# A hand-planned attention and MoE kernel: v loaded in two pieces in the last batch, the planner's rule for adding transfers, and the order of the last matmuls

## The chip, the core and the metric

The kernel runs on one core of a Trainium2 chip. Its engines work side by side: TensorE (PE) multiplies matrices, VectorE (DVE) and ScalarE (ACT) work on tiles, GpSimd (POOL) and SyncE (SP) here mostly start transfers. Each engine takes its own instructions in the order in which the program gives them. The metric is the time of one execution in microseconds (us), and the program computes everything in float32 accuracy, most products split into a high and a low part.

## The reference, cut to what matters

```python
def _attn_ref(q, k, v, tau):            # B, N, C = 4, 6080, 256
    qn = q / (np.linalg.norm(q, axis=1, keepdims=True) + 1e-06)
    kn = k / (np.linalg.norm(k, axis=1, keepdims=True) + 1e-06)
    s = kn.transpose(0, 2, 1) @ qn / tau
    a = softmax(s)                      # over the last axis, written out
    return v @ a

def _moe_ref(x, w_in, w_out):           # x: all 24320 rows; 256 -> 2048 -> 256
    h = x @ w_in
    g = h - np.tanh(h)
    return g @ w_out
```

## The kernel before, in words

**Stages.** There are four batches. Attention is over the 256 channels, so a batch's softmax gives a 256 x 256 matrix, which is multiplied into w_in once (the "folded" factors f, kept in DRAM as f_d). After that every batch is only h = f v, g = h - tanh(h), out = w_out g. The 6080 columns of v make six pairs of two chunks (512 and 512, one pair 512 and 448); the 2048 hidden rows make eight quads. A step of the main loop is one quad of one pair: names such as `c11_3_2_1` are the operand, batch 3, pair 2, quad 1. While a batch runs, the scores of the next are worked out beside it.

**Products of a quad.** A quad multiplies 2 x 2 blocks by a scheme with seven products instead of eight (p1 to p7 in `Quad.product`). Each product is three matmuls of 512 columns (low and high parts). The results gather in PSUM in X, Y and Z: p1 starts X, and p6, p7 and p4 add to X one after the other. Between these, ScalarE copies X out (p1, u2, u3, line L1151), VectorE adds (c11, c22, c12, line L1161: c11 = p1 + Z), then come tanh, the subtraction from h, and the split into a high part (ACT) and a low part (DVE). PE may not add the next product to X before ScalarE has copied it. In the last batch, from pair 1 on ("halves"), Y and Z share a PSUM bank, so that p5 (writes Y) has to wait until c11 has read Z.

**v.** A pair's v comes as four rows of 512 columns per partition (`Moving.load`, L926, tile vraw, one buffer). From it seven operands are made: v0, v2 and v6 are copies of the rows 0, 3 and 2, the others are made from sums (tile vt). Each is split by a CAST on ACT (L952) and a subtraction on DVE (L955). For pairs 2 to 5 of the last batch the load is put at the start of quad 1 of the pair ahead.

**Adding transfers ("joins").** In the last batch the subtraction h - tanh(h) of two results per quad (n11 and t12) is not done by DVE: ACT writes -tanh(h), and a transfer that POOL starts adds h to it (L1176, L1281).

**Second products.** The finished g tiles go into a list, `stream`, and their matmuls (w_out g) are taken from it between the products of later quads. The tables ORDER, UNEVEN and HALVES say how many (a number counts matmuls of 512 columns) behind which product; `lag` says how many are held back. What is left at the end is sorted once more: entries of the last LAST quads that belong to the second chunk go last. Then the outputs are copied out of PSUM and stored.

**The planner.** All this is not run in the order of the code. `plan.add` notes each operation with its engine, a cost, what it reads and writes and, with `after`, the matmul behind which it may start. `Plan.order` then plays the operations through with these costs: PE in its given order, the others by who can start first and whose result is due first, SP's transfers through one modelled queue ("DMA"). The start times that come out set the order of the instructions on every engine. The waits themselves are put in afterwards from the tiles that an instruction really touches; a wrong cost makes a late order, not a wrong result.

Two or three places in this planner matter here. For a load, a reader is held to see its data `LONG_LAG` after the modelled queue is through with it. For an adding transfer, a reader is held to see it JOIN_LAG after its issue, and the queue is occupied for JOIN_SHARE. And a reader depends only on the buffers that stand in its `reads`.

Of the kernel before, what the change touches and what calls it, by code (L numbers as in the profile page):

```python
# [18 lines left out]
P = 128  # L19
# [22 lines left out]
UNEVEN = [  # L42
    ("p6", [2]), ("p2", ["c"]), ("p5", []), ("p7", [12]), ("p3", ["a"]), ("p4", ["d", 3]), ("p1", ["b", 7]),
]
HALVES = [
    ("p6", []), ("p2", [5, "c"]), ("p5", []), ("p7", [5]), ("p4", ["d", 3]), ("p3", ["a", 4]), ("p1", ["b", 5.5]),
]
HALF = NMAX // 2
LAST = 1
SHARE = 1  # L50
JOINED = [(),(11,12)]
SUMS_AT = 3 * 8
ENTER = 10
EARLY = 6
FILLS = 35
# [45 lines left out]
class Plan:  # L101
# [9 lines left out]
    FILL = 0.1  # L111
    WAIT, URGENT, FRONT = 0.35, 2.0, 140.0
    LONG_LAG, BUSY = 4.5, 180.0
    JOIN_LAG, JOIN_SHARE = 4.5, 1.45

    def __init__(self):
        self.ops = []
# [42 lines left out]
    def order(self):  # L160
        ops = self.ops
        for op in reversed(ops):
            if op.due is None:
                op.due = 1e9
            for d in op.deps:
                if d.engine != "PE" or d.fill:
                    d.due = min(1e9 if d.due is None else d.due, op.due - d.cost - self.LAG[d.engine] - self.HOP - d.lag)
        waits = [len(op.deps) for op in ops]
        known = [0.0] * len(ops)
        for op in ops:  # L170
            for d in op.deps:
                d.then.append(op)

        pe = [[op for op in ops if op.engine == "PE" and op.fill == fill] for fill in (False, True)]
        at = [0, 0]
        free = dict.fromkeys(self.ENGINES + ("port", "DMA"), 0.0)
        ready = {e: [op for op in ops if op.engine == e and not waits[op.i]] for e in self.ENGINES if e != "PE"}

        def start(op):
            t = max(free[op.engine], known[op.i])  # L180
            if op.port:
                t = max(t, free["port"])
            if op.engine == "SP":
                t = max(t, free["DMA"] - self.DMA_DEPTH / self.DMA_RATE)
            for b in op.allocs:
                held = b.ring.held
                n = sum(1 for x in op.allocs[:op.allocs.index(b)] if x.ring is b.ring)
                k = len(held) + n - b.ring.bufs
                if k >= 0:
                    if k >= len(held) or held[k].left:  # L190
                        return None
                    t = max(t, held[k].free)
            return t

        done = []
        while len(done) < len(ops):
            best = None
            for i, row in enumerate(pe):
                if at[i] < len(row) and not waits[row[at[i]].i]:
                    op = row[at[i]]  # L200
                    t = start(op)
                    if t is not None and (best is None or t < best[0] - self.FILL):
                        best = (t if i else max(t, min(known[op.i] + op.late, t + op.late)), float(i), op.i)
            for e, some in ready.items():
                can = [(t, op.due, op.i) for op in some for t in [start(op)] if t is not None]
                if can:
                    first = min(can)[0]
                    c = min((c for c in can if c[0] <= first + 1e-9), key=lambda c: c[1:])
                    soon = min((x for x in can if x[0] <= first + self.WAIT), key=lambda c: c[1:])
                    if soon[1] < c[1] - self.URGENT and soon[1] > self.FRONT and e != "SP":  # L210
                        c = soon
                    if best is None or c < best:
                        best = c
            assert best is not None, [(e, len(x)) for e, x in ready.items()]
            op = ops[best[2]]
            op.start = best[0]
            end = free[op.engine] = op.start + op.cost
            seen = end + self.LAG[op.engine] + self.HOP + op.lag
            if op.engine == "SP":
                free["DMA"] = max(free["DMA"], end) + op.size / self.DMA_RATE  # L220
                seen = free["DMA"] + (self.DMA_LAG if op.start < self.BUSY else self.LONG_LAG)
            if op.lag:
                free["DMA"] = max(free["DMA"], end) + self.JOIN_SHARE
            if op.port:
                free["port"] = end
            for b in op.allocs:
                b.ring.held.append(b)
                b.free = seen
            for b in op.reads:
                b.left -= 1  # L230
                b.free = max(b.free, seen)
            if op.engine == "PE":
                at[op.fill] += 1
            else:
                ready[op.engine].remove(op)
            for x in op.then:
                waits[x.i] -= 1
                if op.engine != x.engine or op.engine == "SP" or op.lag:
                    known[x.i] = max(known[x.i], seen)
                else:  # L240
                    known[x.i] = max(known[x.i], end if op.engine == "PE" else end + self.LAG[op.engine] + self.SELF)
                if not waits[x.i] and x.engine != "PE":
                    ready[x.engine].append(x)
            done.append(op)
        return sorted(done, key=lambda op: (op.start, op.i))
# [6 lines left out]
def dve_cost(n):  # L252
    return 0.068 + n * 0.001042
# [11 lines left out]
def attn_moe(ctx: ExitStack, tc: tile.TileContext, qk, v4, qkT, tau, w_in, w_out, outT):  # L265
# [42 lines left out]
    def sb(pool, tag, shape, dtype, name):  # L308
        return pool.tile(list(shape), dtype, tag=tag, name=name, bufs=ring[tag].bufs)
# [42 lines left out]
    class Convert:  # L352
# [5 lines left out]
        def load(self):  # L358
            self.raw = sb(qk_p, "raw", [P, 2, WN], I32, f"raw_{self.name}")
            self.h, self.l = self.dst()  # L360
            nc.sync.dma_start(self.raw, self.src)
# [550 lines left out]
    class Moving:  # L912
# [7 lines left out]
            self.n = self.ns[0]  # L920
            self.hi, self.lo = {}, {}

        def load(self):
            n, s0 = self.n, self.s0
            self.raw = sb(v_p, "vraw", [P, 4, NMAX], F32, f"vraw_{self.b}_{self.p}")
            nc.sync.dma_start(self.raw[:, :, 0:n], v4[self.b, :, 2 * s0:2 * s0 + 4 * n].rearrange("p (a n) -> p a n", a=4))  # L926

        def sums(self, i):
            n = self.n
# [156 lines left out]
    moving = {}  # L1086
    vbuf = {}

    def plan_moving(i, after=()):
        v = moving[i] = Moving(i // NP, i % NP)  # L1090
        n = v.n
        raw, t = Buf(ring["vraw"]), Buf(ring["vt"])
        plan.add("SP", 0.35, v.load, writes=[raw], after=after, size=1.05)
        for j in range(3):
            plan.add("DVE", dve_cost(n if j else 2 * n), lambda j=j: v.sums(j), reads=[raw], writes=[t])
        vbuf[i] = {}
        for j in range(7):
            h = Buf(ring[v.tag(j)])
# [395 lines left out]
        if gs % SLOTS >= NS2:  # L1494
            task(gs - 2, "start", lambda gs=gs: load_folded(gs))
    for i in range(1, B * NP):
        task(NS2 * i - (NS2 - 1 if halved(i // NP, i % NP) and i % NP > 1 else 5), "start", lambda i=i: plan_moving(i, [plan.last_pe]))

    def plan_softmax(a, sq, ps):

# [284 lines left out]
    for gs in range(TOTAL):  # L1785
# [4 lines left out]
        if halves_from - 4 <= gs < halves_from:  # L1790
            lag += 3
        if gs == halves_from:
            lag += 2
        if before and not uneven:
            lag += ENTER if gs < halves_from else 0
            stream[-2:] = reversed(stream[-2:])
# [83 lines left out]
```

## Time and profile before

| | before |
|---|---|
| median of the runs | 2145.4 us (lowest 2145.1) |
| the profiled execution | 2144.87 us |
| its span, first to last instruction | 2143.1 us |
| PE busy | 2135.9 us, 10026 matmuls |
| DVE busy | 1879.0 us |
| ACT busy | 1616.3 us |
| POOL busy | 106.2 us |
| DMA, mean over the span | 196 GB/s |

The profile names each engine's busy time as a share of the span and, for each wait, the instruction or transfer that ended last before the waiting one could go. Matmuls overlap in their pipeline, so that their listed durations (some 0.39 us) are longer than the distance from one start to the next (0.23 us for 512 columns); for the pace of PE the starts are to be read. The same holds on ACT and DVE in a smaller measure: a cast of 512 columns is listed with 0.62 us, and the next one starts 0.52 us later.

### The profile page before, as it was taken

What the parts mean: (1) busy time and instruction counts of PE and PEld (TensorE: products, weight loads), DVE (VectorE), ACT (ScalarE), POOL (GpSimd) and SP (SyncE); (2) the same over time, 40 slices, a digit from 0 to 9 for tenths busy, and PEclk for the clock granted to TensorE, in tenths of its full rate; (3) what the DMA queues carried; (4) which work ended last, traced back from release to release, by engine and by line L of the source; (5) the groups of instructions that cost most, each with busy time, mean ns of one, the idle gap of its engine ahead of it and who ended that gap; (6) DMA issues with size and microseconds to landing.
All of it is one profiled execution on the core that took longest, in us unless ns stands there. A gap on an engine that the chain in (4) does not pass through costs nothing.

```text
span 2143.1 us, 29494 instructions
## 1 busy us (share of the span) xinstructions
PE 2135.9 (100%) x10026; PEld 1802.5 (84%) x10026; DVE 1879.0 (88%) x3332; ACT 1616.3 (75%) x3015; POOL 106.2 (5%) x117
## 2 busy tenths in 40 slices
PE   9999999999999999999999999999999999999999
PEld 8888888888888888888888888888888888888887
DVE  8998988998898888888899888888888998988987
ACT  6677878767777787886777788887676777777776
POOL 5100000000000000000000000000000011111111
PEclk9999999999999999999999999999999999999999
DMA  9845676555335575643533567564353467877874
GB/s 384 303 165 194 214 253 222 189 181 184 127 135 187 212 245 212 219 162 108 199 138 126 180 231 246 196 227 158 110 197 125 156 207 204 230 230 205 231 209 136
DMA packets 143897, 419.73 MB, mean 196 GB/s; under 512 B 20674, under 2 KB 62914, under 8 KB 140674
## 3 DMA queue, kind: packets, MB, share of 16 engines
q1 hardware_dynamic: 132226, 396.87, 52.5%
q0 software_dynamic: 11520, 20.98, 5.4%
q8 instruction: 79, 1.29, 0.2%
q14 instruction: 72, 0.59, 0.1%
HBM read 329.19 MB, written 66.85 MB: 185 GB/s over the span
## 4 chain that ended last, share of the span: by engine, by line
PE 99%; DMA 1%; DVE 0%; SPq 0%; ACT 0%; issue 0%; ACTq 0%
PE ps_o L1448 43%; PE x L326 25%; PE y L326 12%; PE z L326 7%; PE ps_h L1371 5%; PE ps_s L326 3%; PE ps_s L653 2%; PE ps_s L651 1%; PE ps_w L326 1%; DMA n<-c 0%; DMA vhl<-qk_dram 0%; DVE c L1161 0%; DVE t L1285 0%; DVE v L955 0%; DVE gl L1293 0%
## 5 line engine op out<-in xcount | busy, mean ns | idle before, releaser
L326 PE MATMUL x<-v,f 128*128 128x512 f32 (+1 forms) x2304 | 628.2, 389 | 0.0
L1448 PE MATMUL ps_o<-gh,wo_h 128*128 128x512 f32 (+1 forms) x1376 | 533.6, 388 | 0.0
L1448 PE MATMUL ps_o<-gh,wo_l 128*128 128x512 f32 (+1 forms) x1376 | 533.5, 388 | 0.0
L326 PEld LDWEIGHTS x<-v,f 128*128 128x128 f32 x2304 | 430.1, 188 | 84.5
L1293 DVE TENSOR_TENSOR gl<-t,gh 128x512 fp32r<-128x512 f32 (+1 forms) x688 | 456.1, 679 | 20.9 <-ACT gh L1289 19.9
L1289 ACT CAST gh<-t 128x512 fp32r<-128x512 f32 (+1 forms) x688 | 412.2, 617 | 34.4 <-DVE t L1285 20.9
L1448 PE MATMUL ps_o<-gl,wo_h 128*128 128x512 f32 (+1 forms) x1376 | 428.0, 388 | 0.0
L1278 ACT ACTIVATE t<-c 128x512 f32<-128x512 f32 x536 | 333.8, 625 | 94.2 <-DVE c L1161 85.1
L1285 DVE TENSOR_TENSOR t<-c,t 128x512 f32<-128x512 f32 (+1 forms) x496 | 333.9, 677 | 24.7 <-ACT t L1278 19.5
L1151 ACT COPY u<-x 128x512 f32<-128x512 f32 (+1 forms) x384 | 221.9, 578 | 163.0 <-PE x L326 159.4
L1161 DVE TENSOR_TENSOR c<-u,y 128x512 f32<-128x512 f32 (+1 forms) x384 | 258.9, 674 | 76.3 <-ACT u L1151 47.9
L326 PE MATMUL y<-v,f 128*128 128x512 f32 (+1 forms) x1152 | 320.6, 387 | 1.1 <-DVE c L1161 1.0
L1448 PEld LDWEIGHTS ps_o<-gh,wo_l 128*128 128x128 f32 x1376 | 258.5, 188 | 51.4 <-DVE ob L1471 0.9
L1448 PEld LDWEIGHTS ps_o<-gl,wo_h 128*128 128x128 f32 x1376 | 258.2, 188 | 51.7 <-DVE gl L1293 0.6
L1448 PEld LDWEIGHTS ps_o<-gh,wo_h 128*128 128x128 f32 x1376 | 258.4, 188 | 49.1
L326 PEld LDWEIGHTS y<-v,f 128*128 128x128 f32 x1152 | 210.2, 188 | 36.2 <-DVE c L1161 1.8
L1161 DVE TENSOR_TENSOR c<-p,z 128x512 f32<-128x512 f32 x192 | 131.7, 686 | 36.3 <-PE z L326 33.5
L326 PE MATMUL z<-v,f 128*128 128x512 f32 x576 | 162.2, 390 | 0.0
L1278 ACT ACTIVATE t<-x 128x512 f32<-128x512 f32 x152 | 90.9, 598 | 92.7 <-PE x L326 91.1
L1285 DVE TENSOR_TENSOR t<-x,t 128x512 f32<-128x512 f32 x152 | 104.9, 690 | 45.4 <-ACT t L1278 44.9
L326 PEld LDWEIGHTS z<-v,f 128*128 128x128 f32 x576 | 108.1, 188 | 23.3 <-DVE t L1285 0.2
L1151 ACT COPY p<-x 128x512 f32<-128x512 f32 x192 | 112.7, 587 | 15.3 <-PE x L326 12.5
(215 smaller groups left out, 2191.4 us busy)
## 6 DMA issues: line engine op xcount, KB each, us to landing
f<-f_d SPq DMA_DIRECT2D x160, 896.0 KB, 4.6
raw<-qk_dram SPq DMA_DIRECT2D x104, 384.0 KB, 5.0
nt<-qkT_dram SPq DMA_DIRECT2D x96, 380.0 KB, 5.1
f_d<-f SPq DMA_DIRECT2D x32, 896.0 KB, 3.9
vraw<-v_dram SPq DMA_DIRECT2D x24, 1024.0 KB, 7.9
outT_dram<-ob SPq DMA_DIRECT2D x88, 256.0 KB, 3.2
sl<-so_d SPq DMA_DIRECT2D x40, 512.0 KB, 3.3
wt<-wt_d SPq DMA_DIRECT2D x24, 512.0 KB, 6.8
```

Of the source, the lines that this page charges most:

```text
L326: ins = nc.tensor.matmul(out, w, x, start=first and i == 0, stop=last and i == len(seq) - 1, skip_group_check=True,)
L651: nc.tensor.matmul(self.ps[:, 0:C], x[:, 1, k], x[:, 0, q], start=False, stop=last, skip_group_check=True)
L653: nc.tensor.matmul(self.ps.rearrange("p (a c) -> p a c", a=2), x[:, 0, k], x[:, :, q], start=first, stop=False, skip_group_check=True,)
L1151: nc.scalar.copy(self.tiles[to], self.tiles["X"][:, 0:n])
L1161: nc.vector.tensor_add(self.tiles[i], self.tiles[u], self.tiles[ps][:, 0:n])
L1278: nc.scalar.activation(self.tiles["t", i], self.tiles[c][:, 0:n], AF.Tanh, scale=-1.0 if apart else 1.0)
L1285: nc.vector.tensor_sub(x, self.tiles[c][:, 0:n], x)
L1289: nc.scalar.copy(self.g[i][0], self.tiles["t", i])
L1293: nc.vector.tensor_sub(self.g[i][1], self.tiles["t", i], self.g[i][0].bitcast(F32))
L1371: nc.tensor.matmul(outs[b, p, place][:, at_ * HALF:(at_ + 1) * HALF], weights(a, part), quad.g[name][x][:, half * HALF:(half + 1) * HALF], ...
L1448: nc.tensor.matmul(outs[key + (m,)][:, 0:n], (wo_l if part else wo_h)[:, f, m * P:(m + 1) * P], quad.g[i][x], start=first and j == 0, stop ...
```

## The change

It has five parts. (1) In the planner, a reader of an adding transfer is held to see it no earlier than JOIN_AFTER = 2.8 behind the modelled queue's end. (2) For pairs 2 to 5 of the last batch v is loaded in two transfers of two rows each: the first at the start of quad 1 of the pair ahead, the second at the start of quad 2. The operations that make the seven operands are planned with the second (`plan_split`). (3) In the table HALVES half a matmul is moved from behind p4 to behind p2, and `lag` grows by 3 instead of 2 at the start of the halves. (4) LAST is 2 instead of 1. (5) SUMS_AT is 32 instead of 24: the sums of w_out's blocks are made in pair 4 of the first batch instead of pair 3.

```diff
-    ("p6", []), ("p2", [5, "c"]), ("p5", []), ("p7", [5]), ("p4", ["d", 3]), ("p3", ["a", 4]), ("p1", ["b", 5.5]),
+HALVES = [("p6",[]),("p2",[5.5,"c"]),("p5",[]),("p7",[5.0]),("p4",["d",2.5]),("p3",["a",4]),("p1",["b",5.5])]
-LAST = 1
+LAST = 2
+PARTS = [(1,"start"),(2,"start")]
-SUMS_AT = 3 * 8
+SUMS_AT = 32
-    JOIN_LAG, JOIN_SHARE = 4.5, 1.45
+    JOIN_LAG, JOIN_SHARE, JOIN_AFTER = 4.5, 1.45, 2.8
             if op.lag:
                 free["DMA"] = max(free["DMA"], end) + self.JOIN_SHARE
+                seen = max(seen, free["DMA"] + self.JOIN_AFTER)
...
-        def load(self):
+        def load(self, i, k):
             n, s0 = self.n, self.s0
-            self.raw = sb(v_p, "vraw", [P, 4, NMAX], F32, f"vraw_{self.b}_{self.p}")
-            nc.sync.dma_start(self.raw[:, :, 0:n], v4[self.b, :, 2 * s0:2 * s0 + 4 * n].rearrange("p (a n) -> p a n", a=4))
+            if i == 0:
+                self.raw = sb(v_p, "vraw", [P, 4, NMAX], F32, f"vraw_{self.b}_{self.p}")
+            nc.sync.dma_start(
+                self.raw[:, i:i + k, 0:n], v4[self.b, :, 2 * s0 + i * n:2 * s0 + (i + k) * n].rearrange("p (a n) -> p a n", a=k)
+            )
...
-        plan.add("SP", 0.35, v.load, writes=[raw], after=after, size=1.05)
+        plan.add("SP", 0.35, lambda: v.load(0, 4 // parts), writes=[raw], after=after, size=1.05 / parts)
+        vparts[i] = v, raw, t, [Buf(f"vraw{i}_{k}") for k in range(1, parts)]
+        if parts == 1:
+            plan_split(i)
+
+    def plan_part(i, k, after):
+
+        v, raw, t, more = vparts[i]
+        n = 4 // (len(more) + 1)
+        plan.add("SP", 0.35, lambda: v.load(k * n, n), writes=[more[k - 1]], after=[*after, raw.writers[0]], size=1.05 / (len(more) + 1))
+        if k == len(more):
+            plan_split(i)
+
+    vparts = {}
+
+    def plan_split(i):
+        v, raw, t, more = vparts[i]
+        n = v.n
         for j in range(3):
-            plan.add("DVE", dve_cost(n if j else 2 * n), lambda j=j: v.sums(j), reads=[raw], writes=[t])
+            plan.add("DVE", dve_cost(n if j else 2 * n), lambda j=j: v.sums(j), reads=[raw, *more], writes=[t])
         vbuf[i] = {}
         for j in range(7):
             h = Buf(ring[v.tag(j)])
             l = Buf(f"vl{i}_{j}", h)
             src = t if v.PLACES[j][0] else raw
             plan.add("ACT", act_cost(v.width(j)), lambda j=j: v.split_hi(j), reads=[src], writes=[h])
...
-        task(NS2 * i - (NS2 - 1 if halved(i // NP, i % NP) and i % NP > 1 else 5), "start", lambda i=i: plan_moving(i, [plan.last_pe]))
+        late = halved(i // NP, i % NP) and i % NP > 1
+        parts = PARTS if late else [(NS2 - 5, "start")]
+        for k, (at_, place) in enumerate(parts):
+            task(
+                NS2 * (i - 1) + at_, place,
+                lambda i=i, k=k, n=len(parts): plan_part(i, k, [plan.last_pe]) if k else plan_moving(i, [plan.last_pe], n),
+            )
...
         if gs == halves_from:
-            lag += 2
+            lag += 3
```

Every matmul of the kernel before is in the kernel after. Three places show how the rows move.

**ScalarE, last batch, pair 2, around quad 2.** `v0`, `v2`, `v6` with `_3_3` are the operands of the next pair's v; `u2`, `u3` are the copies of X between the products; `n11`, `t22`, `t12` are tanh; `ghb1`, `gh22` and the other CASTs are high parts. Before:

```order
L1151 COPY p1_3_2_2_19077<-x_3_2_2_19065 128x512
L1209 CAST ghb1_3_2_1_19086<-n11_3_2_1_19002 128x256
L1278 ACTIVATE t22_3_2_1_19091<-c22_3_2_1_19027 128x512
L952 CAST v0_3_3_19101<-vraw_3_3_18972 128x512
L1151 COPY u2_3_2_2_19108<-x_3_2_2_19065 128x512
L1289 CAST gh22_3_2_1_19113<-t22_3_2_1_19091 128x512
L1209 CAST t1_3_2_1_19123<-ts_3_2_1_19081 128x512
L1173 ACTIVATE n11_3_2_2_19134<-c11_3_2_2_19117 128x512
L952 CAST v2_3_3_19140<-vraw_3_3_18972 128x512
L1278 ACTIVATE t12_3_2_1_19148<-c12_3_2_1_19058 128x512
L1151 COPY u3_3_2_2_19155<-x_3_2_2_19065 128x512
```

After:

```order
L1171 COPY p1_3_2_2_19076<-x_3_2_2_19065 128x512
L1298 ACTIVATE t22_3_2_1_19086<-c22_3_2_1_19027 128x512
L1298 ACTIVATE t12_3_2_1_19094<-c12_3_2_1_19059 128x512
L1171 COPY u2_3_2_2_19102<-x_3_2_2_19065 128x512
L1229 CAST ghb1_3_2_1_19109<-n11_3_2_1_18997 128x256
L1309 CAST gh22_3_2_1_19115<-t22_3_2_1_19086 128x512
L955 CAST v0_3_3_19125<-vraw_3_3_18971 128x512
L955 CAST v2_3_3_19136<-vraw_3_3_18971 128x512
L955 CAST v6_3_3_19144<-vraw_3_3_18971 128x512
L1193 ACTIVATE n11_3_2_2_19147<-c11_3_2_2_19112 128x512
L1171 COPY u3_3_2_2_19153<-x_3_2_2_19065 128x512
```

The three casts of v, which were spread (v6 came behind u3), stand together now, ahead of n11 and u3.

**SyncE's queue at the same place.** `f` is a quad's folded factor, `sl` sums of w_out's blocks, `outT_dram` the output of the pair ahead. Before:

```order
L909 DMA f_163_18969<-f_d3_3_17364 128x1792
L926 DMA vraw_3_3_18972<-v4_dram 128x2048
L494 DMA sl_161_19000<-so_d1_116 128x1024
L1474 DMA outT_dram<-ob_3_1_1_1_19032 128x512
L1474 DMA outT_dram<-ob_3_1_1_0_19048 128x512
L1403 DMA outT_dram<-ob_3_1_0_18998 128x512
L1403 DMA outT_dram<-ob_3_1_1_19034 128x512
L909 DMA f_164_19099<-f_d3_4_17472 128x1792
L494 DMA sl_162_19138<-so_d2_117 128x1024
```

After:

```order
L909 DMA f_163_18964<-f_d3_3_17364 128x1792
L927 DMA vraw_3_3_18971<-v4_dram 128x1024
L494 DMA sl_161_19006<-so_d1_116 128x1024
L1494 DMA outT_dram<-ob_3_1_1_1_19048 128x512
L1494 DMA outT_dram<-ob_3_1_1_0_19046 128x512
L1423 DMA outT_dram<-ob_3_1_0_19004 128x512
L1423 DMA outT_dram<-ob_3_1_1_19034 128x512
L909 DMA f_164_19092<-f_d3_4_17472 128x1792
L927 DMA vraw_3_3_18971<-v4_dram 128x1024
L494 DMA sl_162_19138<-so_d2_117 128x1024
```

The first piece has the place of the whole load, and the second stands behind the four stores and the next f.

**VectorE, last batch, pair 1, around quad 2.** `ts` and `glb1` read the joined tile n11 of quad 1; c11 of quad 2 is the addition that frees the bank of Z. Before:

```order
L1234 TENSOR_TENSOR ts_3_1_1_18131<-n11_3_1_1_18056 128x256
L1234 TENSOR_TENSOR ts_3_1_1_18131<-n21_3_1_1_18105,n11_3_1_1_18056 128x256
L1285 TENSOR_TENSOR t22_3_1_1_18136<-c22_3_1_1_18080,t22_3_1_1_18136 128x512
L1214 TENSOR_TENSOR glb1_3_1_1_18156<-n11_3_1_1_18056,ghb1_3_1_1_18145 128x256
L1214 TENSOR_TENSOR t1_3_1_1_18150<-ts_3_1_1_18131,t1_3_1_1_18150 128x512
L1161 TENSOR_TENSOR c11_3_1_2_18169<-p1_3_1_2_18127,z_3_1_2_18152 128x512
```

After:

```order
L1305 TENSOR_TENSOR t22_3_1_1_18131<-c22_3_1_1_18082,t22_3_1_1_18131 128x512
L1254 TENSOR_TENSOR ts_3_1_1_18150<-n11_3_1_1_18054 128x256
L1181 TENSOR_TENSOR c11_3_1_2_18160<-p1_3_1_2_18126,z_3_1_2_18145 128x512
L1234 TENSOR_TENSOR glb1_3_1_1_18170<-n11_3_1_1_18054,ghb1_3_1_1_18157 128x256
L1313 TENSOR_TENSOR gl22_3_1_1_18178<-t22_3_1_1_18131,gh22_3_1_1_18163 128x512
```

c11 was the sixth of these rows and stands behind one reader of n11 now.

## Rows read from the trace of the kernel before

**Rows 1.** The page, busy time: us, share of the span, instructions.
```profile
PE 2135.9 (100%) x10026; PEld 1802.5 (84%) x10026; DVE 1879.0 (88%) x3332; ACT 1616.3 (75%) x3015; POOL 106.2 (5%) x117
```

**Rows 2.** All of PE's listed waits: us in total, times, longest.
```profile
PE idle L1823 <- DVE ones L318: 1.1, 1, 1.1
PE y L326 <- DVE c L1161: 1.0, 1, 1.0
PE ps_s L326 <- DMA vhl<-qk_dram: 0.5, 1, 0.5
```

**Rows 3.** The chain that ended last, in order of time: start, us, what.
```profile
1740.28 7.21 DMA n<-c
```

**Rows 4.** Timeline of PE, 1748 to 1755: start, us, instruction, [idle before <- releaser].
```profile
1749.06 0.40 PE L1371 MATMUL ps_h<-t,wo_h 128*128 128x256 f32 x2
1750.47 0.96 PE L326 MATMUL y<-v,f 128*128 128x512 f32 x3 [1.00 <-DVE c L1161]
...
1753.23 0.84 PE L326 MATMUL x<-v,f 128*128 128x512 f32 x3
```

**Rows 5.** Timeline of SP's issues, 1814 to 1833: start, us of issuing.
```profile
1824.60 1.35 SPq L1474 DMA_DIRECT2D outT_dram<-ob  x2
1827.14 0.81 SPq L1403 DMA_DIRECT2D outT_dram<-ob  x2
1828.05 0.41 SPq L909 DMA_DIRECT2D f<-f_d  x1
1831.18 0.33 SPq L494 DMA_DIRECT2D sl<-so_d  x1
```

**Rows 6.** Line L909, the one f issued at 1828.05.
```profile
DMA to landing us min/median/max: 5.4/5.4/5.4
```

**Rows 7.** Line L494, the one sl issued at 1831.18.
```profile
DMA to landing us min/median/max: 3.5/3.5/3.5
```

**Rows 8.** Line L494, the one sl issued at 1725.05, directly behind an f.
```profile
DMA to landing us min/median/max: 5.2/5.2/5.2
```

**Rows 9.** Line L909, the one f issued at 1744.0, behind four stores.
```profile
L909 SPq DMA_DIRECT2D f<-f_d x1: 799/799/799, 1744.0 to 1744.0; - x1
...
DMA to landing us min/median/max: 6.8/6.8/6.8
```

**Rows 10.** Line L494, the one sl issued at 1811.0, alone.
```profile
DMA to landing us min/median/max: 3.2/3.2/3.2
```

**Rows 11.** Timeline of ACT, 1827.5 to 1834.
```profile
1829.54 0.59 ACT L1151 COPY u<-x 128x512 f32<-128x512 f32 x1
...
1831.06 0.63 ACT L1173 ACTIVATE n<-c 128x512 f32<-128x512 f32 x1
1831.59 0.61 ACT L952 CAST v<-vraw 128x512 fp32r<-128x512 f32 x1
...
1832.81 0.59 ACT L1151 COPY u<-x 128x512 f32<-128x512 f32 x1
```

**Rows 12.** Timeline of PE, 1831 to 1835: the products on v4 (p7) and v5 (p4).
```profile
1831.92 0.85 PE L326 MATMUL x<-v,f 128*128 128x512 f32 x3
...
1833.88 0.84 PE L326 MATMUL x<-v,f 128*128 128x512 f32 x3
```

**Rows 13.** Timeline of all engines, the end.
```profile
2137.54 0.39 PE L1448 MATMUL ps_o<-gl,wo_h 128*128 128x512 f32 x1
...
2137.99 0.42 DVE L1400 TENSOR_TENSOR ob<-eh,s 128x256 f32<-128x256 f32 x1
...
2138.33 0.69 DVE L1471 COPY ob<-ps_o 128x512 f32<-128x512 f32 x1
...
2139.26 0.84 SPq L1474 DMA_DIRECT2D outT_dram<-ob  x2
```

**Rows 14.** Stretches behind the last matmul: us, busy (PE, PEld, DVE, ACT, POOL), granted clock, DMA.
```profile
2138.70:2142.60 3.90, 0.00 (x0) 0.00 (x0) 0.32 (x1) 0.53 (x1) 0.00 (x0) 1.00 0.70 269
2142.70:2143.10 0.40, 0.00 (x0) 0.00 (x0) 0.00 (x0) 0.00 (x0) 0.00 (x0) 0.50 0.00 0
```

More of the change, by code (lines that the diff above doesn't have):

```diff
@@ L44 @@
 ]
-HALVES = [
-    ("p6", []), ("p2", [5, "c"]), ("p5", []), ("p7", [5]), ("p4", ["d", 3]), ("p3", ["a", 4]), ("p1", ["b", 5.5]),
-]
+HALVES = [("p6",[]),("p2",[5.5,"c"]),("p5",[]),("p7",[5.0]),("p4",["d",2.5]),("p3",["a",4]),("p1",["b",5.5])]
 HALF = NMAX // 2
-LAST = 1
+LAST = 2
 SHARE = 1
 JOINED = [(),(11,12)]
-SUMS_AT = 3 * 8
+PARTS = [(1,"start"),(2,"start")]
+SUMS_AT = 32
 ENTER = 10
@@ L1087, in attn_moe, with plan_moving @@
     vbuf = {}
-    def plan_moving(i, after=()):
+    def plan_moving(i, after=(), parts=1):
         v = moving[i] = Moving(i // NP, i % NP)
```

## Prediction

> **What bounds the kernel now.** I read first the busy times: TensorE (PE) works through the whole span of 2143.1 us [rows 1]. Busy is not the same as never waiting, so I read next what PE waited for: three waits long enough to be listed, 2.6 us in all, two of them at the start-up (on the constant `ones` and on the first rows of q and k) [rows 2]. From there to the last batch PE waits for nothing, so no other engine's work there has a price as long as it stays hidden. The third wait is in the last batch. The chain of work shows what led to it: an adding transfer (n<-c) that took 7.21 us from its issue at 1740.28 [rows 3]. VectorE and ScalarE work strictly in their order, both had an instruction on that transfer's result at the head, and the addition that PE needed stood behind it: PE's last ps_h matmuls started at 1749.06, about 0.25 us of work, and the next product only at 1750.47, 1.2 us late [rows 4]. That, and the last stores after the last matmul, is all that can be gained. The number of matmuls does not change.
>
> **A wait that goes.** In the order shown for VectorE, the addition c11 of quad 2 now stands right behind the first instruction on the joined tile and ahead of the other readers of it. It is then done before PE asks for it: minus 1.2 us. If the transfer still lands late, the gain is nothing; the first piece of v is half as large, so there is less ahead of it, and I take all of the 1.2.
>
> **A wait that comes.** The second piece of v holds the last two of the four rows, and operands v2 and v6 are made from exactly these (PLACES: rows 3 and 2). But plan_split lets the ScalarE casts depend on `raw` alone, that is, on the first piece; only VectorE's sums name `more`. So the planner sets the casts as if the first piece were enough, and the order shows it: v0, v2, v6 stand in one block, ahead of the tanh n11 and of the copy u3. The real wait of v2 is on the second piece, and ScalarE cannot pass it. Behind it is u3, which must take X out of PSUM before PE's product p4 may add to X again. So PE waits too.
>
> How long: I work it out at quad 2 of pair 2 (1828 to 1834 us), in the clock of the kernel before.
> - Issue. The second piece stands right behind the load of f, itself behind four output stores [rows 5]. f is issued at 1828.05 and holds the queue 0.41, so the piece goes at 1828.46.
> - Landing. f landed 5.4 after its issue, at 1833.4 [rows 6]. The sl load has the size of one piece (512 KB): it was issued at 1831.18 behind that f and took 3.5 [rows 7], landing at 1834.7, 1.2 to 1.3 behind f. The piece takes that place in the queue: 1834.6, 6.1 us after its issue. Bounds: an sl issued directly behind an f without the stores took 5.2 [rows 8], which gives 1833.7; the slowest such load that I found, an f behind four stores and a v load, took 6.8 [rows 9], which gives 1835.3; an sl with nothing in front took 3.2 [rows 10], which gives 1831.7. I take 1834.6, the row of this place.
> - ScalarE before it. In the order after, behind u2 (1829.54) stand ghb1, gh22 and v0; at about 0.5 us each [rows 11] v2 is reached near 1831.4 and waits some 3.2 us.
> - ScalarE after it. From the landing to the end of u3: v2, v6 and n11 at 0.53 each (n to v, 1831.06 to 1831.59) and u3 at 0.59 [rows 11], 2.2 us with a little for the hand-over: 1836.8.
> - PE. Between the product on v4 (1831.92) and p4 (1833.88) lies other PE work [rows 12], which the order after keeps up to 0.1 us. So PE stands still from 1833.8 to 1836.8: **3.0 us** (2.1 and 3.7 at the bounds 1833.7 and 1835.3, nothing below 1831.6).
>
> PE has no slack in which to win this back. The same rows (v0, v2, v6, n11, u3) stand at quad 2 of pairs 2, 3 and 4, with the same four stores and f ahead of the piece: 3 x 3.0 = 9.0 us.
>
> The fourth place is quad 2 of pair 1, the one where PE waited before. There f was issued at 1744.0 behind four stores and a whole v, and took 6.8 [rows 9]. With 512 KB less ahead (1.2 us by the step from f to sl above) it lands at 1749.6, the piece at 1750.9, u3 ends at 1753.1. PE would come to p4 at 1753.23 less the 1.2 us that are saved [rows 4], 1752.0: a new wait of 1.1 us, between nothing and 2.
>
> **The end.** The last PE work on the bank of the first output half ends near 2137.95, but its copy on VectorE starts at 2138.33, behind the additions for the first chunk (the last at 2137.99), and the two last stores are issued together from 2139.26 [rows 13]. With the last two quads' first chunk ahead, six matmuls more lie behind these additions; the copy starts about 0.4 us earlier and the two stores no longer wait on each other: minus 0.4 us (nothing to 0.6).
>
> **At nothing.** The eight Sums (moved from quads 24 to 31 to quads 32 to 39 of the first batch), the halves of a matmul moved in HALVES, the lag of one more, the four more DMA issues of SP (0.4 us each on a queue that idles between its rows [rows 5]): what hides them is that PE has no wait between the start-up and the last batch [rows 2]. Without that cover each would cost a wait of the kind that rows 4 show, about 1 us where it falls.
>
> **Sum.** -1.2 + 9.0 + 1.1 - 0.4 = +8.5 us. The profiled execution took 2144.9 us (its span is 2143.1), which makes 2153.4; the median of the runs shown, 2145.4, is 0.5 above it. I say **2153.7 us**, 0.4% slower, which is far below the 2% that a measurement of this kernel is held to tell from no change.
>
> **Rivals.**
> 1. *The change does what it says, and not slower.* The second piece lands before ScalarE asks. The point is 1831.6, 3.1 us after issue; then only the gains stay: 2145.4 - 1.2 - 0.4 = 2143.8. For it: a 512 KB load alone took 3.2 [rows 10]. Against it: f is directly in front and alone needs until 1833.4 [rows 6]. Chance 8%. The Trainium skill ("DMA: Bandwidth & Descriptors", section "Anatomy of one DMA — SWDGE (gpsimd) path") gives a transfer about 2.0 us fixed plus bytes over 436 GB/s; for a piece that is 3.2 us by my estimate, which is this rival's side, and the rows agree for a load alone and disagree behind an f.
> 2. *The queue is longer than I take it.* Stores, f, piece and an adding transfer now come within a few microseconds. At a landing of 1835.3 or later the three places cost 3.7 to 4.5 each and the fourth 2: +11.5 to +14, 2157 to 2160. For it: the 7.21 and the 6.8 [rows 3, 9]. Against: at this place f took 5.4, not 6.8 [rows 6, 9], and the first piece is smaller than the whole v was. Chance 15%.
> 3. *The clock falls in the waits.* After the last matmul the granted clock stayed at 1.00 (2.4 GHz) through 3.9 us without matmuls and was 0.50 (1.2 GHz) after that [rows 14]. My waits are shorter. If it fell nevertheless, and stayed low for as long as PE had waited (an estimate), half of that is lost: 1.5 us more at three places, 2158. Chance 7%. The Trainium skill ("TensorE: Matmul & The Clock Gate", section "HAM oscillation — how this bites in real kernels") tells of kernels in which PE's waits for DMA lower the clock again and again; by that rule this rival is the time. No row of this kernel shows it in mid-run.
>
> **How the numbers follow.** My forecast, 2150 to 2157, has 66%; rivals 1, 2, 3 have 8, 15 and 7; 4% are left for pieces that land a little earlier than 1833.7 (2146 to 2149). From 2148 to 2160 all but rival 1, the tails of 2 and half of the 4% lie inside, some 85%. All cases are within 2% of 2145.4 (2102.5 to 2188.3): same 0.98, faster 0.005, slower 0.015 for something unseen.
>
> **What would show it.** In the profile after: a ScalarE cast v<-vraw (v2) that waits for DMA vraw<-v_dram at four places some 82 us apart, about 3 us each; at each, PE waiting for ScalarE's u before an x product, 3 us thrice and about 1 us in pair 1; no PE wait for VectorE's c near 1749. If the casts do not wait, or PE reaches p4 without a gap, the forecast is wrong in its main step; if the gaps are there with another length, the landing is the term that is off; if the matmuls after a gap run at a granted clock of 0.5, it is rival 3.

## The result, and the profile after it

The changed kernel takes **2167.5 us** (2167.0 to 2168.8), the kernel before 2145.3: a ratio of 1.0106, interval 1.0086 to 1.0126. It is 1.1% slower; the forecast was 2153.7, range 2148 to 2160. The profiled execution has a span of 2167.0 us (before 2143.1), so 23.9 us are to be found. (The profiled execution is the longest of the four; by the medians the change costs 22.2 us.)

What PE waited for (us in total, times, longest), the answer to [rows 2]:

```profile
core 0 of [0], span 2167.0 us
engine line waited for: us in total, times, longest us
PE x L326 <- ACT u L1171: 16.3, 4, 5.4
PE ps_o L1468 <- ACT ob L1491: 1.1, 1, 1.1
PE idle L1849 <- DVE ones L318: 1.1, 1, 1.1
PE ps_s L326 <- DMA vhl<-qk_dram: 0.5, 1, 0.5
```

The wait for VectorE's c11, the third of [rows 2], is gone. Four waits for ScalarE's copy u stand in its place, where they were forecast, and one for ob, the copy of a finished output out of PSUM, that was not. Two rows of ScalarE's waits in the last batch show who held it:

```profile
ACT v L955 <- DMA vraw<-v_dram: 17.9, 4, 5.8
...
ACT gh L1309 <- DMA t<-c: 2.9, 3, 2.5
```

The issue of the second piece by SyncE, and ScalarE, at quad 2 of pair 2 (start, us, instruction, idle before it and what ended that), the answer to [rows 11]:

```profile
1829.76 0.45 SPq L927 DMA_DIRECT2D vraw<-v_dram  x1
...
1831.07 0.62 ACT L955 CAST v<-vraw 128x512 fp32r<-128x512 f32 x1
1837.16 1.14 ACT L955 CAST v<-vraw 128x512 fp32r<-128x512 f32 x2 [5.47 <-DMA vraw<-v_dram]
1838.21 0.62 ACT L1193 ACTIVATE n<-c 128x512 f32<-128x512 f32 x1
1838.74 0.56 ACT L1171 COPY u<-x 128x512 f32<-128x512 f32 x1
```

v0 is cast at 1831.07; then ScalarE stands for 5.5 us at v2 until the second piece lands at 1837.16, 7.4 us after its issue, and only then come v2 and v6, n11, and u3. TensorE at the same place, the answer to [rows 12]:

```profile
1833.88 0.40 PE L1468 MATMUL ps_o<-gh,wo_h 128*128 128x512 f32 x1
1839.36 1.65 PE L326 MATMUL x<-v,f 128*128 128x512 f32 x3 [5.08 <-ACT u L1171]
```

The other two such places read 4.96 and 5.40. The second pieces there:

```profile
DMA to landing us min/median/max: 8.1/8.1/8.1
```

```profile
DMA to landing us min/median/max: 7.5/7.5/7.5
```

The second of the PE rows has something more: three matmuls of an x product take 1.65 us where [rows 12] have 0.85. The stretches behind the three waits (us; busy time and count of PE, PEld, DVE, ACT, POOL; granted clock; DMA) say why:

```profile
1838.20:1844.90 6.70, 5.54 (x15) 4.48 (x16) 4.09 (x7) 4.39 (x9) 0.86 (x1) 0.50 0.33 65
1926.95:1933.70 6.75, 5.91 (x15) 4.77 (x16) 4.46 (x8) 4.09 (x8) 0.86 (x1) 0.50 0.38 75
2015.70:2022.45 6.75, 5.63 (x15) 4.57 (x16) 4.18 (x7) 4.36 (x9) 0.89 (x1) 0.50 0.31 57
```

The granted clock fell to 0.50 (1.2 GHz) while PE stood (these stretches begin before PE goes on), and PE worked through 5.54, 5.91 and 5.63 us at half pace: half of each is lost, 2.8, 3.0 and 2.8.

**The account.** Waits at the three places 5.08 + 4.96 + 5.40 = 15.4; the clock behind them 8.5; the fourth place 16.3 - 15.4 = 0.9; the wait for ob 1.1. Off that go the wait for c11, 1.0 [rows 2], and 0.5 at the end: the last matmul begins 4.4 us before the end of the span, where it was 4.9 before (rows of before, then after). That is +24.4.

```profile
2138.22 0.39 PE L1448 MATMUL ps_o<-gl,wo_h 128*128 128x512 f32 x1
```

```profile
2162.60 0.39 PE L1468 MATMUL ps_o<-gl,wo_h 128*128 128x512 f32 x1
```

A further gain shows in how many matmuls fall between 400 and 500 us of the span, first before and then after:

```profile
400.00:500.00 100.00, 100.00 (x440) 82.06 (x439) 95.64 (x182) 74.46 (x137) 0.00 (x0) 1.00 0.47 159
```

```profile
400.00:500.00 100.00, 100.00 (x443) 82.81 (x442) 94.06 (x180) 74.37 (x135) 0.00 (x0) 1.00 0.49 159
```

Three matmuls more, at 0.2 us each 0.6 us: the Sums, on VectorE from 342 to 449 us before, stand from 448 to 530 now, and small gaps that VectorE had made in PE's work near 440 are gone. One of them, in the kernel before: VectorE does a Sum (so) ahead of gl, and PE's weight load (PEld) waits for gl.

```profile
437.12 0.68 DVE L485 TENSOR_TENSOR so<-ss,so 128x512 fp32r<-128x512 f32 x1
```

```profile
438.46 0.30 PEld L1448 LDWEIGHTS ps_o<-gl,wo_h 128*128 128x128 f32 x2 [0.36 <-DVE gl L1293]
```

Every run below that has the Sums at their new place counts 443 here, those with the old place 440 or 441. 24.4 - 0.6 = 23.8, against 23.9 measured. That the two agree to 0.1 us is in part luck: behind the start-up PE is 0.2 us ahead of the kernel before, which is not in the account and differs from run to run (0.5 ahead to 0.9 behind in those below).

### The profile page after: what moved, and what is told of

It reads as the page before. It is cut to its first block, busy times and chain, and to the rows that moved or that the text cites. A ratio compares the mean times of both kernels' runs of the same rounds, so it can differ in the third digit from the quotient of the medians.

```text
span 2167.0 us, 29512 instructions
## 1 busy us (share of the span) xinstructions
PE 2143.7 (99%) x10026; PEld 1808.2 (83%) x10026; DVE 1879.5 (87%) x3332; ACT 1614.4 (75%) x3015; POOL 106.4 (5%) x117
## 4 chain that ended last, share of the span: by engine, by line
PE 96%; DMA 2%; ACT 0%; issue 0%; DVE 0%; SPq 0%; POOL 0%; ACTq 0%; POOLq 0%
PE ps_o L1468 42%; PE x L326 24%; PE y L326 12%; PE z L326 6%; PE ps_h L1391 4%; PE ps_s L326 3%; PE ps_s L653 2%; DMA vraw<-v_dram 1%; PE ps_s L651 1%; PE ps_w L326 1%; DMA vhl<-qk_dram 0%; DMA t<-c 0%; ACT n L1193 0%; ACT v L955 0%; ACT u L1171 0%
## 5 line engine op out<-in xcount | busy, mean ns | idle before, releaser
L326 PE MATMUL x<-v,f 128*128 128x512 f32 (+1 forms) x2304 | 631.2, 391 | 16.3 <-ACT u L1171 16.3
L1309 ACT CAST gh<-t 128x512 fp32r<-128x512 f32 (+1 forms) x688 | 412.4, 617 | 35.4 <-DVE t L1305 20.4
L1468 PE MATMUL ps_o<-gl,wo_h 128*128 128x512 f32 (+1 forms) x1376 | 422.6, 388 | 0.0
```

The source lines that it names most:

```text
L326: ins = nc.tensor.matmul(out, w, x, start=first and i == 0, stop=last and i == len(seq) - 1, skip_group_check=True,)
L1309: nc.scalar.copy(self.g[i][0], self.tiles["t", i])
L1468: nc.tensor.matmul(outs[key + (m,)][:, 0:n], (wo_l if part else wo_h)[:, f, m * P:(m + 1) * P], quad.g[i][x], start=first and j == 0, stop ...
```

## Experiments

Two questions stood: is the whole loss ScalarE at the cast v2, or do the pieces cost something in themselves; and why is a place worth 8 us and not 3. Ratios are against runs of the kernel before that were made along with them on the same chip (2145.0 to 2145.3). What is said of waits and of the clock is read from one profiled execution of each.

| run | us | ratio, interval |
|---|---|---|
| e1_named | 2147.2 | 1.0008 (0.9999 to 1.0017) |
| e2_one_load | 2147.1 | 1.0009 (1.0000 to 1.0018) |
| e3_pieces_alone | 2157.8 | 1.0060 (1.0046 to 1.0074) |
| e4_turning | 2160.6 | 1.0072 (1.0058 to 1.0086) |
| e5_no_t12_join | 2158.6 | 1.0063 (1.0049 to 1.0077) |
| e6_piece_earlier | 2150.4 | 1.0024 (1.0015 to 1.0034) |
| c1_later_reader | 2144.1 | 0.9994 (0.9986 to 1.0003) |
| c2_old_order | 2144.6 | 0.9999 (0.9990 to 1.0008) |
| d_join_after | 2145.5 | 1.0001 (0.9992 to 1.0010) |
| d_last | 2144.2 | 0.9996 (0.9986 to 1.0005) |

### The missing name: e1_named

```diff
-            src = t if v.PLACES[j][0] else raw
+            src = [t] if v.PLACES[j][0] else [raw, *more] if v.PLACES[j][1] > 1 else [raw]
...
```

> The changed kernel with one edit: the casts and splits of v2 and v6 are planned as readers of the second piece of v as well, so that the planner sets them by its landing; two pieces, join lag, LAST, HALVES and the Sums stay. Theory A (all of the loss is ScalarE standing at the cast v2, and what follows from it in PE): no wait of a ScalarE cast for DMA vraw<-v_dram over 1 us, no PE wait for ScalarE's u, granted clock 1.00 through the last batch, and the time falls by about 24 us to 2143 to 2144.5, at or a little below the kernel before. Rival B (pieces, a longer DMA queue or the new order cost time in themselves): the time stays above 2155, with other waits of 2 us and more in the last batch.

2147.2 us: 20.4 of the 22 us are back by this line (the two lines behind it, which take the list, are left out here). It changes no instruction, only where the planner sets the casts and subtractions of v and what follows from that in the order. ScalarE's list of waits has no vraw any more, the granted clock is 1.00 throughout the last batch, and PE's waits are:

```profile
PE x L326 <- ACT p L1171: 2.9, 3, 1.1
PE idle L1849 <- DVE ones L318: 1.1, 1, 1.1
PE ps_o L1468 <- ACT ob L1491: 1.0, 1, 1.0
```

Theory A holds for the bulk; rival B is out. But the time is 2.7 us above the top of what was expected, and PE has three new waits, for the copy p. (The interval of the ratio reaches down to 0.9999, so that what is left is read from these waits and not from the time alone.) ScalarE ahead of the first of them:

```profile
1835.06 0.62 ACT L1229 CAST b<-n 128x512 fp32r<-128x512 f32 x1 [0.24 <-DVE n L1209]
1837.50 0.62 ACT L1309 CAST gh<-t 128x512 fp32r<-128x512 f32 x1 [1.83 <-DMA t<-c]
1838.03 0.58 ACT L1171 COPY p<-x 128x512 f32<-128x512 f32 x1
```

The adding transfer t<-c of this place took 8.8 us from issue to landing; its first reader gh stands ahead of p, waits, and p and PE wait with it. c1 and c2 below take this up.

### One load again: e2_one_load

```diff
-PARTS = [(1,"start"),(2,"start")]
+PARTS = [(1,"start")]
```

> The changed kernel with v in one load again (PARTS with one entry), everything else of the change kept. Theory A: the two pieces bring the whole loss, so the time is 2143 to 2145.5, with no PE wait over 2 us in the last batch; the wait of 1.2 us near 1749 stays away if the planned adding transfers remove it by themselves. Rival C (the adding transfers planned ahead, by another order, bring part of the loss): 2150 or more, with PE waits for u or c of some us.

2147.1 us: without the second piece the large loss is gone as well, and the wait for c11 stays away, so neither the planned adding transfers nor the order bring the large loss. It is 1.6 us above what theory A allowed, by one wait for ob and the slow work behind it (PE timeline, then the stretches in and behind the wait):

```profile
1746.19 0.61 PE L1468 MATMUL ps_o<-gh,wo_l 128*128 128x512 f32 x1 [2.00 <-ACT ob L1491]
```

```profile
1744.20:1746.10 1.90, 0.00 (x0) 0.00 (x0) 0.35 (x1) 1.50 (x3) 0.00 (x0) 1.00 1.06 330
1746.50:1749.80 3.30, 3.30 (x10) 2.72 (x10) 2.21 (x4) 2.22 (x4) 0.00 (x0) 0.50 0.85 288
```

A wait of 2.0 us was enough for the clock to fall behind it: 3.3 us at half pace, 1.65 lost. Not in every execution: of the ten timed, the four with a mean granted clock of 1.000 take 2145.6 to 2147.0, the six with 0.999, of which the profiled one is the longest, 2147.0 to 2148.3. The prediction had taken waits below the 3.9 us of [rows 14] for nearly safe.

### The pieces on the kernel before: e3_pieces_alone

```diff
-            plan.add("SP", 0.35, v.load, ...)
+            ... (in words) two loads of two rows, as in the change; HALVES, LAST, lag, SUMS_AT as before; no JOIN_AFTER
```

> The kernel before with one part of the change: v in two pieces in the last batch, the casts planned as readers of the first piece alone, as in the changed kernel; HALVES, LAST, the Sums and the lag of adding transfers as before. In its order the tanh n11 and the adding transfer stand ahead of v2. Theory A with the mis-sized landing (the adding transfer started at the same moment as the piece makes it late): the piece lands about 6 us after its issue, PE waits 2 to 3 us at three places, the granted clock stays at 1.00, and the time is 2150 to 2154. Rival D (pieces alone account for the whole loss, whatever stands ahead of v2): 2164 to 2168, with PE waits over 4 us and a granted clock of 0.50 behind them.

2157.8 us, 4 above the range of theory A and 6 below that of rival D. In this order ScalarE does n11 and t12 first, and the adding transfers are issued 2.6 us and more behind the piece, not with it. The pieces land 6.1, 6.3 and 5.7 us after issue at the three places, where the prediction had 6.1, and PE's waits are 2.76, 1.96 and 1.99 us. What was missed is again the clock: it fell behind the first and the third, not behind the second (the stretches from the fall on, or from PE's going on where it did not fall).

```profile
1835.60:1842.42 6.82, 6.03 (x16) 4.87 (x17) 4.58 (x8) 4.14 (x8) 0.10 (x1) 0.50 0.68 156
```

```profile
1922.20:1929.00 6.80, 6.80 (x37) 5.89 (x38) 6.24 (x12) 6.20 (x12) 0.89 (x1) 1.00 0.75 202
...
2006.30:2009.60 3.30, 3.30 (x11) 2.62 (x10) 2.79 (x5) 2.06 (x4) 0.00 (x0) 0.50 0.59 97
```

### The clock apart from the wait: e4_turning

```diff
+                if to == "X" and a == A22 and self.b == B - 1 and self.s == 2 and self.p in (2, 3, 4):
+                    for _ in range(12):
+                        nc.tensor.matmul(outs[self.b, self.p, 7][:, HALF:HALF + P], ones, ones, start=False, stop=True, skip_group_check=True)
```

> The changed kernel with 12 matmuls more (128 columns, 32-bit, about 0.2 us each, 2.6 us in all) ahead of the product p4 of quad 2 in pairs 2, 3 and 4, into a half of a PSUM bank that nothing reads then; they stand in the stretch in which PE waits. Nothing is left out. Theory E (the slow matmuls behind each wait come from the clock, which falls because PE stands idle for over 4 us): the idle stretches are 2.5 to 3 us, the granted clock stays at 1.00, and the time falls by 3 x 2.7 = 8 us to about 2159. Rival F (the matmuls are slow behind the wait for another reason, such as PSUM or SBUF traffic): the same time as the changed kernel, 2167, or a little more.

2160.6 us (2157.8 to 2162.7), 7 below the changed kernel, although it does 36 matmuls more; the profiled execution is the shortest of the four, with a span of 2156.0, 11.0 below. PE's timeline and the stretches at the first place (each of the twelve is listed as two):

```profile
1834.17 2.84 PE L1158 MATMUL ps_h<-ones 128*128 128x128 f32 x24
1838.68 0.96 PE L326 MATMUL x<-v,f 128*128 128x512 f32 x3 [1.67 <-ACT u L1174]
```

```profile
1834.10:1838.70 4.60, 2.93 (x26) 2.70 (x25) 0.04 (x1) 2.21 (x5) 0.18 (x1) 1.00 0.77 235
1838.70:1845.50 6.80, 6.80 (x36) 5.84 (x37) 6.16 (x11) 5.76 (x11) 1.49 (x2) 1.00 0.59 173
```

The product begins 4.7 us after the start of the matmul ahead of the twelve (1833.94; in the changed kernel 5.5, from 1833.88), but the clock stays at 1.00 and the matmuls behind run at full pace. Over the three places the product comes 3 us earlier in all, by pieces that landed earlier; the other 8 of the 11 us are the clock's. So theory E holds in this execution, and how much a run gains depends on the landings too; in the two longest of the four the mean granted clock is 0.999, so that it may have fallen there once. Waits of 1.7 us and less left the clock alone.

### What made the piece late: e5_no_t12_join, e6_piece_earlier

```diff
-            return self.b == B - 1 and i in JOINED[halved(self.b, self.p)]
+            return self.b == B - 1 and i in JOINED[halved(self.b, self.p)] and (i, self.s) != (12, 1)
```

> The changed kernel with one adding transfer per pair less: t12 of quad 1 of the half quads is subtracted by VectorE. The casts still name the first piece alone. In the changed kernel that transfer starts within 0.2 us of the second piece. Theory J (it delays the piece): the piece lands about 6 us after its issue instead of 7.4, PE waits 3 to 4 us instead of 5.1 to 5.6 at three places, and the granted clock falls at fewer of them or stays low for less: 2153 to 2161. Rival K (f and the stores alone make the piece late): landing 7 us and more, 2165 to 2168.

In the changed kernel the adding transfer was issued 0.14 us behind the second piece at the first place, 1.3 behind it at the second and 0.2 ahead of it at the third. Without the transfer ScalarE stood 3.5 us (not 5.5) and got the piece 5.7 us (not 7.4) after its issue at 1829.75:

```profile
1835.49 0.62 ACT L955 CAST v<-vraw 128x512 fp32r<-128x512 f32 x1 [3.54 <-DMA vraw<-v_dram]
```

At the other two places the pieces landed 8.1 and 7.5 us after issue with the transfer, and without it:

```profile
DMA to landing us min/median/max: 6.7/6.7/6.7
```

```profile
DMA to landing us min/median/max: 6.8/6.8/6.8
```

On average 7.7 with and 6.4 without: the adding transfer costs the piece 1.3 us. Counted from the landing of the f ahead, the same shows: the piece comes 2.1 to 2.8 us behind f with it, 1.3 to 1.5 without, and 1.2 was forecast. PE's waits are 2.83, 3.10 and 3.19 us, the 3.0 of the forecast, and still the time is 2158.6, because the clock fell behind all three (the first of them):

```profile
1837.50:1840.80 3.30, 3.30 (x10) 2.56 (x9) 2.23 (x4) 2.79 (x6) 0.36 (x1) 0.50 0.44 79
```

Theory J holds. The Trainium skill ("DMA: Bandwidth & Descriptors", section "Queues, rings and completion order") says that each DMA engine takes turns between the queues that have work for it, packet by packet; by that rule an adding transfer from GpSimd's queue slows a load that SP has already issued, and these rows agree.

```diff
-PARTS = [(1,"start"),(2,"start")]
+PARTS = [(1,"start"),(1,"c")]
```

> The changed kernel with the second piece of v issued earlier: PARTS (1, start), (1, c), that is in quad 1 and not at the start of quad 2, so that it no longer stands behind the load of f. The casts still name the first piece alone. Theory A (the price is the time from ScalarE's asking to the piece's landing, plus the clock behind it): the piece is issued some 2 to 4 us earlier, ScalarE waits 0 to 3 us for it, PE 0 to 2 us at each place, the granted clock stays at 1.00, and the time is 2144 to 2155. Rival B (reading a tile that a second piece still writes costs by itself, wherever the piece stands): 2160 and more.

2150.4 us. The piece now goes 0.5 us ahead of f (2.2 at the third place) and lands 4.7, 4.8 and 5.9 us after issue. It is not issued 2 to 4 us earlier, as expected, but only 0.5 to 1.5 (against PE's work ahead of the wait); most of the gain is that f no longer stands ahead of it. PE waits 1.90, 1.18 and 2.29 us, and the clock fell behind the last alone:

```profile
2001.70:2005.00 3.30, 3.30 (x9) 2.63 (x9) 2.37 (x4) 2.47 (x6) 0.52 (x1) 0.50 1.00 271
```

That too differs between executions: seven of ten have a mean granted clock of 1.000 and take 2149.3 to 2150.7, three, the profiled one among them, 0.999 and 2151.6 to 2152.8. The same missing name costs 5 us in place of 22: the price is that of the wait, with the clock on top of it, from about 2 us on in some executions; rival B is out.

### The two microseconds that were left: c1_later_reader, c2_old_order, d_join_after, d_last

c1 is e1_named with JOIN_AFTER 4.0; c2 is e1_named with the HALVES and the lag of the kernel before.

```diff
-    JOIN_LAG, JOIN_SHARE, JOIN_AFTER = 4.5, 1.45, 2.8
+    JOIN_LAG, JOIN_SHARE, JOIN_AFTER = 4.5, 1.45, 4.0
```

> The changed kernel with the casts named as readers of the second piece (as e1_named), and one number more: JOIN_AFTER 4.0 in place of 2.8, so that the planner expects an adding transfer's sum 1.2 us later and sets its first reader on ScalarE (gh) further back. Theory G (the 2 us that e1_named is above the kernel before are ScalarE standing at gh for an adding transfer that took 8 to 9 us, with the copies ob and p behind it): the PE waits of 1.0 us for ob near 1743 and of 1.0 to 1.3 us for p at three places go, and the time is about 4 us below e1_named, 2142 to 2144. Rival H (these waits come from PE order or from the pieces): the waits stay, 2146 to 2148.

> The changed kernel with the casts named as readers of the second piece (as e1_named), and the PE order of the kernel before: HALVES and the lag of the first half quad (2, not 3) as before. Pieces, JOIN_AFTER, LAST and the Sums stay. If the moved halves and the lag cause the wait for ob near 1743 (in the prediction they were set at nothing), that wait of 1.0 us goes, and at most the waits for p (1.0 to 1.3 us at three places) stay or shrink: 2143 to 2146. If the order has no part in it: as e1_named, 2147.

Both medians are 2.6 to 3.1 us below that of e1_named (on another chip; the intervals of the ratios overlap), c1's at the top of what was expected. PE's waits in c1, all of them:

```profile
PE idle L1849 <- DVE ones L318: 1.1, 1, 1.1
PE x L326 <- ACT p L1171: 0.4, 1, 0.4
```

In c1 the copies ob and p stand ahead of gh; in c2 ob does near 1743, and gh waits at most 0.6 us. By these waits theory G holds, and so does c2's first branch: with JOIN_AFTER 2.8 the moved halves and the lag put gh ahead of the copies, and either number mends it (HALVES and the lag were not taken apart). The spans of their profiled runs, 2141.5 and 2141.2, are about what is left of 2143.1 when the three gains (1.0, 0.5, 0.6) come without a wait; but these executions are the second shortest and the shortest of eleven. Timed they are at 0.9994 and 0.9999: neither is shown to be faster than the kernel before.

The next two are the kernel before with one part each.

```diff
+                seen = max(seen, free["DMA"] + self.JOIN_AFTER)
```

> The kernel before with one part of the change: JOIN_AFTER (2.8), the planner's wait for an adding transfer behind the queue. One load of v, HALVES, LAST, lag and Sums as before. By the prediction's step this removes the wait of 1.2 us for c near 1749 and nothing else changes: 2143.5 to 2144.3, 0.05% faster. Rival: it sets gh too early as in e1_named, ScalarE stands there and hands PE a wait for p or ob in its place: 2145 or more.

2145.5 us, a miss: the wait for c11 went, as the step said, and small ones came elsewhere, so that nothing was gained. Much as its rival had it, ScalarE stands at gh for an adding transfer some 11 us later, and PE behind it loses about 1.6 us against the kernel before within 7 us, more than the two waits that are listed:

```profile
1761.21 0.62 ACT L1309 CAST gh<-t 128x512 fp32r<-128x512 f32 x1 [1.98 <-DMA t<-c]
```

```profile
1761.88 0.50 PE L1468 MATMUL ps_o<-gh,wo_l 128*128 128x512 f32 x1 [0.25 <-ACT gh L1309]
...
1765.21 0.98 PE L326 MATMUL y<-v,f 128*128 128x512 f32 x3 [0.25 <-DVE c L1181]
```

```diff
-LAST = 1
+LAST = 2
```

> The kernel before with one part of the change: LAST = 2, the first chunk of the last two quads ahead. By the prediction's step on the end the two last stores no longer wait on each other, and the stretch behind the last matmul is about 0.4 us shorter than before (4.5 us there); the wait of 1.2 us for c near 1749 stays; 2144.5 to 2145.2. Rival: the stretch is as long as before, so that the 0.5 us gained in the changed kernel came from elsewhere.

2144.2 us; the last matmul begins at 2138.05, 4.15 us before the end of the span of 2142.2, against 4.9 before (2138.22 to 2143.1). The gain is LAST's own, 0.7 in this profile; the timed ratio of 0.9996 does not show it beyond its interval.

```profile
2138.05 0.39 PE L1468 MATMUL ps_o<-gl,wo_h 128*128 128x512 f32 x1
```

## Why the prediction was wrong

- **The wait at the cast v2: right.** The cause (plan_split lets the casts depend on the first piece), the four places, the chain v2, v6, n11, u3, p4, and ScalarE's arrival (1831.4 forecast, 1831.7 measured) came as worked out; e1_named shows that this one dependency is the loss. From landing to the end of u3 it took 2.1 us (forecast 2.2).
- **The landing: mis-sized.** The term was 6.1 us after issue, from an sl behind an f [rows 7]. It measured 7.4, 8.1 and 7.5. In the changed kernel an adding transfer is issued 0.6 us behind f and 0.14 behind the piece (both below), since the change itself moves t12's transfer there. e5 gives the piece 6.4 without it, e3 5.7 to 6.3 with adding transfers some 3 us behind. The rows taken for the bounds had other neighbours: the sl of [rows 8] had no adding transfer near it, that of [rows 7] had one 0.9 us behind it, 4.0 behind f, and the f of [rows 9] one that had started 3.8 us earlier. None had both an f and an adding transfer started within 1.5 us of it, as the pieces have at all three places, so 6.8 was too low. The rival that gave 3.2 us for a piece alone [rows 10] was furthest off. The three waits are 15.4 us instead of 9.0: +6.4. Some 4.7 of that is the landing. The other 1.8 is the issue: the piece went out 4.5, 5.4 and 4.3 us before PE ran out of work, where the forecast had 5.3 (1828.46 to 1833.8). At the first place the two stores ahead of f took 1.61 us to issue (0.81 in [rows 5]), at the third f took 1.43 (0.41); why is open.
POOL's issues here, before and then after:

```profile
1832.05 0.86 POOL L1176 DMA_DIRECT2D n<-c  x1 [9.34 <-ACT n L1173]
```

```profile
1829.90 0.86 POOL L1301 DMA_DIRECT2D t<-c  x1 [6.89 <-ACT t L1298]
```

- **The clock: the step that failed, 8.5 us put at nothing.** It stood among the rivals with 7 in 100, because "My waits are shorter" than the 3.9 us of [rows 14]. That row shows how late the clock fell once, not how early it can: in e3 it was down 2.0 us after PE had stopped (1833.63 to 1835.60). In mid-run, over the profiled executions, it fell behind all seven PE waits of 2.7 us and more, behind three of the five between 1.9 and 2.3, and behind none of 1.7 or less. With the landing right the forecast would still have missed by 5 us: e5 has the waits as forecast and takes 2158.6, what rival 3 gave (2158). Either error alone would have left the time near 2159, inside the range of 2148 to 2160 (2167.5 less the 8.5 of the clock is 2159.0); the two together took it out. The Trainium skill ("TensorE: Matmul & The Clock Gate", section "HAM oscillation — how this bites in real kernels") tells of a kernel whose clock falls in every wait for a DMA; here the trace agrees for the three waits of 5 us behind the second piece, and not for the 0.9 us of the fourth place.
- **The fourth place** (1.1 us): 0.9. **The wait that goes** (1.2): gone, 1.0 by the list of waits.
- **HALVES and the lag "at nothing": wrong by 1.1 us, together with JOIN_AFTER.** The cover named was that PE has no wait between the start-up and the last batch. The halves begin in the last batch itself, where that cover does not hold: PE waits for ob, which stands behind gh on ScalarE, and gh waits for an adding transfer. By c1, c2 and d_join_after it takes both the moved halves with the lag and JOIN_AFTER at 2.8 to bring this.

```profile
1743.11 0.62 ACT L1309 CAST gh<-t 128x512 fp32r<-128x512 f32 x1 [2.51 <-DMA t<-c]
```

```profile
1744.70 0.50 PE L1468 MATMUL ps_o<-gh,wo_l 128*128 128x512 f32 x1 [1.08 <-ACT ob L1491]
```

- **The Sums "at nothing": wrong by 0.6 us, a gain.** The gaps that they made were too short to be listed among PE's waits [rows 2]; the count of matmuls shows them.
- **The end** (0.4): 0.5 in the changed kernel, 0.7 with LAST alone.

Sum by the measured terms: -1.0 + 15.4 + 8.5 + 0.9 + 1.1 - 0.5 - 0.6 = +23.8.

## What to carry to other kernels

When a load is cut in two, every reader has to be named for the piece that it reads: the waits that are put in afterwards keep the result right, and hide the error as time. A wait of the matmul engine in mid-run has two prices, its length and the half-pace work behind it; here the second came in some executions from about 2 us on and in every profiled one from 2.7, so count both, and don't take one late fall of the clock for a bound. A transfer's time is taken from a row that has the same neighbours, those of the other queues too, in the order after the change.

## What was not expected of the hardware

- The clock fell behind waits as short as 2.0 us, not behind others of 1.90 and 1.96 us, and once (e3, third place) more than a microsecond after PE had gone on. In e2 and e6 it fell in some executions and not in others of the same program. No run here separates what decides between them.
- The low clock lasted unequally: at least 6.7 us from its fall within the waits of about 5 us, some 3.3 at most of the shorter ones, and 6.8 at one of 2.76 us.
- An adding transfer of 256 KB (t<-c) took 8.7 us beside f, a piece and an sl; the median of its kind in the changed kernel is 4.2.
- Most changed versions, e2 with its one load among them, spread more from run to run (c1: 2142.8 to 2146.2) than the kernel before beside them (2144.4 to 2146.4 in 27 runs); in e2 and e6 part of that is the clock, for c1 it was not looked into.
